# Sparse attention and SwiGLU on one core: batch 2's q and k transposed by PE, later casts and transposes at other places, six output buffers

## The chip, the cores and the metric

The kernel runs on one core of a Trainium2 chip. Five engines work side by side: PE (matmuls, with PEld for its weight loads), DVE (elementwise work), ACT (activations), POOL and SP. In this kernel POOL mostly starts transfers that gather or cast, and SP starts plain transfers and crossbar transposes. Each engine takes its instructions in program order and waits on semaphores for the others. The metric is the device time of one execution in microseconds (us). The kernel before takes 384.35 us, the median of 3 runs (383.87 to 388.22).

## The reference

There are 8 batches of 576 tokens with 8 heads of 64. A token attends to the tokens within 32 places of it; 8 global tokens attend to all and are attended to by all. The result, 4608 tokens of 512 values, goes through a gated feed-forward block.

```
scores = q @ k.T / sqrt(D)                       # per batch and head, 576 x 576
mask   = |i - j| <= 32  or  i is global  or  j is global
attn   = softmax(where(mask, scores, -1e9))
x      = (attn @ v), heads side by side           # 4608 x 512
out    = (silu(x @ w_gate) * (x @ w_val)) @ w_out # 512 -> 1536 -> 512
```

## The kernel before

The feed-forward block is cut into nine **chunks** of 512 tokens. A chunk is 16 **units**: 12 gate units (`gate`, L643: eight matmuls for `pg` and `pv`, then tanh on ACT and two products on DVE that give `h`) and 4 output units (`outp`, L692: twelve matmuls into `po`, a copy by ACT into an `osb` buffer, a transfer by SP to `out`). The units are numbered through from 0; chunk c holds units 16c to 16c + 15.

The attention of a batch is a list of small steps, and these are put into the **gaps** behind the units: `gaps[n]` runs after unit n (L707 to L744). So PE always has feed-forward matmuls between two attention steps. This order, written out by hand, is the order of instructions on every engine. A chunk needs the attention of the tokens that it covers: chunk 3, tokens 1536 to 2047, needs the first 320 tokens of batch 3 (its tiles 0, 1 and 2).

The steps of one batch:

- `step_T` (L330, batches 0 and 1 only): PE transposes k and q of two heads, 24 small transposes. ACT copies the k half into `kT`, DVE the q half into `qT`.
- `step_GT`, `step_S2`, `step_SG`: the global tokens. S2 gives `p2` (global queries), SG gives `pg` (global keys).
- `step_P2T` (L407): `p2` transposed. Batches below XB = 3 do it on PE with an ACT copy; the others by a crossbar transpose started on SP (`p2t`, L410).
- `step_AV2` (L420): the output of the global queries, from `p2t` and `va`.
- `step_S(u)`: banded scores, exp on ACT, band mask on DVE. `step_AV(tp)` and `step_AV8`: the values, then a normalisation on DVE that gives `xa`.
- `step_X(tp)` and `step_X8`: `xa` transposed into `xT`, the feed-forward block's input. Below XB by PE, from XB on by a crossbar transpose on SP (L542, L564).

The inputs of a batch come in three ways. q and k of batches 0 and 1 are loaded and cast by POOL into `k_bf` and `q_bf` (`load_qk_part`, L76; one buffer of each), for `step_T`. q and k of batches 2 to 7 are cast by POOL into a bf16 copy in DRAM with heads side by side (`cast_qk`, L105), and SP transposes the copy into `kT` and `qT` through the crossbar (`transpose_qk`, L113). v goes into `va` by POOL (`load_v`, L96, five blocks; two `va` buffers, so batch b waits for the AV steps of batch b - 2), and SP copies it shifted into `vb` (L123). The rows of the global tokens come by two indirect transfers (`gather`, L221) that POOL then masks (`gather_mask`, L232), waiting for them to land.

For batch b >= 1 the function `later` (L585), at the end of the scores of batch b, starts the transposes of batch b + 2, then gather and mask of batch b + 2 and the cast of batch b + 3; `later_v` does `load_v` of batch b + 2. Batch 2's cast is queued at the very start, behind the weights (L283), its transposes at unit 14, and those of batch 3 at unit 15. Batch 2's steps stand at units 19 to 30, batch 3's from unit 31, batch b's from unit 16(b - 1) - 1.

Work tiles have few buffers: `osb` three (pool `ffnw`, L69), `kT` and `va` two each, `qT` two. PSUM has one double bank for scores (`psc`), one for the rest of attention (`pm`), and four banks for the feed-forward block (`pf`).

Of the kernel before, what the change touches and what calls it, by code (L numbers as in the profile page):

```python
# [9 lines left out]
FP32 = mybir.dt.float32  # L10
# [7 lines left out]
P = 128  # L18
# [8 lines left out]
def kernel(  # L27
# [13 lines left out]
    B, H, S, D = q.shape  # L41
    NG = global_idx.shape[0]
    DM, DF = moe_w_gate.shape
# [7 lines left out]
    LP = 96  # L51
    LJ = S // LP
    KC = S + 2 * WIN
    XB = 3
    STEP = {2: 1.0, 3: 1.08, 4: 1.08, 5: 1.1, 6: 1.1, 7: 1.1}
    W = D + 2

    assert (B, H, S, D, NG, DM, DF) == (8, 8, 576, 64, 8, 512, 1536)
# [78 lines left out]
    loaded = [None] * B  # L137
# [116 lines left out]
    kqms = [None] * B  # L254
# [23 lines left out]
    for i in range(4):  # L278
# [1 line left out]
            out=wo_sb[:, 3 * i : 3 * i + 3, :],  # L280
            in_=moe_w_out[3 * P * i : 3 * P * (i + 1), :].rearrange("(fc p) m -> p fc m", p=P),
        )
    cast_qk(2)  # L283


    mg = const.tile([P, S], BF16)
    mg2 = const.tile([P, KC], BF16)
# [28 lines left out]


    def attention(b):
        ld = loaded[b]
        kT = kT_bufs[b % 2]  # L320
        va = va_bufs[b % 2]
        st = {}
# [7 lines left out]
        def step_T(hp):  # L330
            if hp == 0:
                qTs[b] = bp.tile([P, HP, S], BF16, tag="qT", name="qT")
            if b > 0:
                pool, tag = (pm, "m") if hp == 3 else (psc, "sc")
                pair = pool.tile([P, 2, 1024], BF16, tag=tag, name="ps_t")
            pss = []
            for n, name in enumerate(("k", "q")):
                if b == 0:
                    ps = pf.tile([P, LJ, LP], BF16, tag="f", name="ps_t")
                else:  # L340
                    ps = pair[:, n, 0:S].rearrange("p (j i) -> p j i", j=LJ)
                pss.append(ps)
                src = ld[name]
                for j in range(LJ):
                    for par in range(2):
                        nc.tensor.transpose(  # L346
                            out=ps[64 * par : 64 * par + 64, j, :],
                            in_=src[:, 2 * hp + par, D * j : D * (j + 1)],
                            identity=ident[0:LP, 0:LP],
                        )  # L350
# [4 lines left out]
            nc.vector.tensor_copy(  # L355
                out=qTs[b][:, hp, :].rearrange("p (i j) -> p i j", j=LJ),
                in_=pss[1].rearrange("p j i -> p i j"),
            )
# [46 lines left out]
            nc.vector.tensor_tensor(out=st["p2"], in0=pe, in1=mg2, op=ALU.mult)  # L405

        def step_P2T():  # L407
            if b >= XB:
                st["p2t"] = work.tile([P, 5, P], BF16, tag="p2t", name="p2t")
                nc.sync.dma_start_transpose(out=st["p2t"], in_=st["p2"])  # L410
                return
            ps = mtile([P, 5, P], BF16, "ps_p2t")
            for u in range(5):
                nc.tensor.transpose(
                    out=ps[:, u, :], in_=st["p2"][:, P * u : P * (u + 1)], identity=ident
                )
            st["p2t"] = work.tile([P, 5, P], BF16, tag="p2t", name="p2t")
            nc.scalar.copy(out=st["p2t"], in_=ps)
# [163 lines left out]
        def vb():  # L582
            st["vb"] = load_vb(b)

        def later():  # L585

            if b + 2 < B:
                transpose_qk(b + 2)
                kqms[b + 2] = gather_mask(*gather(b + 2))
            if b + 3 < B:  # L590
                cast_qk(b + 3)

        def later_v():
            if b + 2 < B:
                load_v(b + 2)

        L = lambda f, *a: (lambda: f(*a))
        if b == 0:
            return [
# [5 lines left out]
            ], [L(step_S, 4)], [L(step_AV8), later_v], [L(step_X8)]  # L605
        mid = [
            [L(step_S2), L(step_SG)],
            [L(step_P2T), L(step_S, 0)],
# [6 lines left out]
            [L(step_X, 3), L(step_S, 4), later],  # L615
        ]
        end = [[L(step_AV8), later_v], [L(step_X8)]]
        if b == 1:
            return [
                [L(step_GT)], [], [], [], [L(step_T, 0)], [L(step_T, 1)],  # L620
                [L(step_T, 2), L(step_T, 3), vb],
            ] + mid, end
        if b < XB:
            return [[L(step_GT), vb]] + mid + end
        return [
            [L(step_GT), vb],
            [L(step_S2), L(step_SG)],
# [6 lines left out]
            [L(step_S, 4), L(step_AV, 2), L(step_X, 2), later],  # L634
            [L(step_AV, 3), L(step_AV8), L(step_X, 3), L(step_X8), later_v],
        ]


    def ffn(t0, n):
# [52 lines left out]
        def outp(ts):  # L692
            po = pf.tile([P, DM], FP32, tag="f", name="po")
            for fc in range(NFC):
# [1 line left out]
                    out=po, lhsT=st["h"][:, fc, P * ts : P * (ts + 1)], rhs=wo_sb[:, fc, :],  # L696
                    start=(fc == 0), stop=(fc == NFC - 1),
                )
            osb = ffnw.tile([P, DM], FP32, tag="osb", name="osb")
            nc.scalar.mul(out=osb, in_=po, mul=0.5)  # L700
            r0 = t0 + P * ts
            nc.sync.dma_start(out=out[r0 : r0 + P, :], in_=osb)
# [14 lines left out]
    gaps = dict(enumerate(first))  # L717
    for i, g in enumerate([s4, av8, x8]):
        gaps[1 + i] = g + gaps[1 + i]
    gaps[8].append(lambda: kqms.__setitem__(2, gather_mask(*gather(2))))  # L720
    gaps[10].append(lambda: cast_qk(3))
    gaps[14].append(lambda: transpose_qk(2))
    for i, g in enumerate(last):
        gaps[16 + i] = g
    at = 19.0
    for b in range(2, B):
        steps = attention(b)
        need = (512 - 64 * b + P - 1) // P
# [47 lines left out]
```

## Time and profile before

| | |
|---|---|
| median of 3 runs | 384.35 us |
| the profiled execution, its own time | 384.5 us |
| its span, first to last instruction | 382.8 us |
| mean granted TensorE clock | 0.991 |
| DVE busy | 235.3 us (61%) |
| POOL queue's transfers (q0) | 19.40 MB in 101472 packets |
| SP queue's transfers (q1) | 24.09 MB in 50320 packets |

A row of the timeline gives start, length, engine, line, operation, and the tiles as output<-input; in brackets stands how long the engine had been idle before and what ended the wait. Rows of matmuls can be merged (x4 is four of them), and some matmul records are missing. Matmuls overlap, so the time that a step takes is read from the start of one row to the start of the next. A row of waits gives the engine and line that waited, what ended the wait, the total in us, how many times, and the longest. A row of groups ends in busy time, mean ns of one, and idle time before with what ended it. SPq and POOLq rows are transfers; "to landing" is the time from issue until the data is there.

The first gate of chunk 1 starts at 73.77 us, of chunk 2 at 118.57, of chunk 3 at 163.54, of chunk 4 at 203.40, of chunk 5 at 240.70, of chunk 6 at 279.20 and of chunk 7 at 316.43.

### The profile page before, as it was taken

What the parts mean: (1) busy time and instruction counts of PE and PEld (TensorE: products, weight loads), DVE (VectorE), ACT (ScalarE), POOL (GpSimd) and SP (SyncE); (2) the same over time, 40 slices, a digit from 0 to 9 for tenths busy, and PEclk for the clock granted to TensorE, in tenths of its full rate; (3) what the DMA queues carried; (4) which work ended last, traced back from release to release, by engine and by line L of the source; (5) the groups of instructions that cost most, each with busy time, mean ns of one, the idle gap of its engine ahead of it and who ended that gap; (6) DMA issues with size and microseconds to landing.
All of it is one profiled execution on the core that took longest, in us unless ns stands there. A gap on an engine that the chain in (4) does not pass through costs nothing.

```text
span 382.8 us, 7690 instructions
## 1 busy us (share of the span) xinstructions
PE 346.2 (90%) x3125; PEld 173.5 (45%) x3175; DVE 235.3 (61%) x469; ACT 147.4 (39%) x228; POOL 99.8 (26%) x114
## 2 busy tenths in 40 slices
PE   2678999979899679988999999999999999999995
PEld 2464545434444235433554454345444544444442
DVE  5774885376844639248944993399458926834750
ACT  2633574336334324144414441354154413323321
POOL 8865751609183052450132012000000000000000
PEclk9999999999999969999999999999999999999999
DMA  8999999999989999999299139940350131011002
GB/s 115 115 197 201 185 201 152 145 180 215 170 76 164 228 60 148 138 237 139 28 148 240 29 34 130 212 58 16 99 134 2 29 86 61 0 49 63 0 29 82
DMA packets 151827, 43.98 MB, mean 115 GB/s; under 512 B 138352, under 2 KB 146032, under 8 KB 151792
## 3 DMA queue, kind: packets, MB, share of 16 engines
q0 software_dynamic: 101472, 19.40, 61.8%
q1 hardware_dynamic: 50320, 24.09, 29.6%
q8 instruction: 25, 0.41, 0.5%
q14 instruction: 10, 0.08, 0.1%
HBM read 38.28 MB, written 16.52 MB: 143 GB/s over the span
## 4 chain that ended last, share of the span: by engine, by line
PE 78%; DMA 11%; DVE 5%; issue 3%; ACT 2%; SPq 0%; POOL 0%; DVEq 0%; ACTq 0%; POOLq 0%
PE po L695 24%; PE pg L650 21%; PE pv L650 20%; DMA p2t<-p 5%; PE ps_av L498 3%; DMA qT<-qf 3%; PE ps_s L454 2%; PE ps_av L507 2%; DMA vb<-va 2%; DMA q_bf<-in_q_dram 1%; PE ps_t L346 1%; PE ps_x L552 1%; DVE h L688 1%; DVE gv L684 1%; ACT pe L462 1%
## 5 line engine op out<-in xcount | busy, mean ns | idle before, releaser
L650 PE MATMUL pv<-xT,wv_sb 128*128 128x512 bf16 x420 | 109.2, 381 | 1.9 <-ACT osb L700 1.4
L650 PE MATMUL pg<-xT,wg_sb 128*128 128x512 bf16 x393 | 106.9, 382 | 3.4 <-DVE gv L684 0.8
L684 DVE SCALAR_TENSOR_TENSOR gv<-th,pg 128x512 bf16<-128x512 bf16 x108 | 73.9, 684 | 52.7 <-ACT th L682 52.3
L682 ACT ACTIVATE th<-pg 128x512 bf16<-128x512 f32 x108 | 64.5, 598 | 89.6 <-PE pg L650 78.8
L695 PE MATMUL po<-wo_sb,h 128*128 128x512 bf16 x417 | 94.0, 379 | 2.1 <-issue 1.9
L688 DVE TENSOR_TENSOR h<-gv,pv 128x512 bf16<-128x512 bf16 x108 | 74.3, 688 | 11.7 <-PE ps_av L507 0.5
L650 PEld LDWEIGHTS <-wv_sb 128*128 128x128 bf16 x424 | 41.7, 98 | 52.4 <-issue 3.1
L695 PEld LDWEIGHTS <-h 128*128 128x128 bf16 x432 | 40.8, 98 | 47.0
L700 ACT ACTIVATE osb<-po 128x512 f32<-128x512 f32 x36 | 21.5, 597 | 93.5 <-PE po L695 74.0
L650 PEld LDWEIGHTS <-wg_sb 128*128 128x128 bf16 x424 | 37.6, 98 | 43.8 <-issue 4.8
L101 POOL DMA_DIRECT2D va<-in_v_dram x40 | 37.1, 1195 | 63.8 <-PE ps_av L507 45.1
L462 ACT ACTIVATE pe<-ps_s 128x1024 bf16<-128x1024 f32 (+1 forms) x40 | 37.6, 940 | 19.7 <-PE ps_s L454 19.7
L467 DVE TENSOR_TENSOR pt<-pe,band 128x1024 bf16<-128x1024 bf16 (+1 forms) x40 | 25.4, 635 | 11.0 <-ACT pe L462 10.3
L485 DVE TENSOR_TENSOR xa<-ps_av,den 128x512 bf16<-128x512 f32 (+1 forms) x40 | 25.5, 638 | 1.4
L479 DVE TENSOR_REDUCE den<-ps_av 128x8 f32<-128x16 f32 (+1 forms) x40 | 6.7, 168 | 29.0 <-PE ps_av L507 27.5
L498 PE MATMUL ps_av<-gvt,pg 128*64 128x264 bf16 x128 | 18.8, 303 | 1.0 <-DVE gvt L439 1.0
L507 PE MATMUL ps_av<-vb,pt 128*64 128x66 bf16 x256 | 18.3, 201 | 1.5 <-DMA vb<-va 1.5
L507 PEld LDWEIGHTS <-pt 128*64 128x64 bf16 x512 | 18.4, 117 | 1.9 <-DMA vb<-va 1.7
L454 PEld LDWEIGHTS <-kT 64*128 64x128 bf16 x576 | 11.5, 98 | 16.2 <-issue 15.4
L507 PE MATMUL ps_av<-va,pt 128*64 128x66 bf16 x256 | 18.5, 201 | 0.0
L454 PE MATMUL ps_s<-qT,kT 64*128 64x64 bf16 x576 | 16.4, 197 | 1.8 <-ACT pe L462 1.3
L235 POOL TENSOR_TENSOR kqm<-kg,mka 128x128 bf16<-128x128 f32 x8 | 3.2, 395 | 54.6 <-DMA kg<-in_k_dram,gofs 54.6
(98 smaller groups left out, 210.3 us busy)
## 6 DMA issues: line engine op xcount, KB each, us to landing
out_dram<-osb SPq DMA_DIRECT2D x36, 256.0 KB, 3.3
vb<-va SPq DMA_DIRECT2D x14, 264.0 KB, 4.3
kf<-in_k_dram POOLq DMA_DIRECT2D x6, 576.0 KB, 10.3
qf<-in_q_dram POOLq DMA_DIRECT2D x6, 576.0 KB, 15.2
va<-in_v_dram POOLq DMA_DIRECT2D x24, 128.0 KB, 9.7
va<-in_v_dram POOLq DMA_DIRECT2D x16, 96.0 KB, 8.9
wg_sb<-in_moe_w_gate_dram POOLq DMA_DIRECT2D x3, 512.0 KB, 7.4
wv_sb<-in_moe_w_val_dram POOLq DMA_DIRECT2D x3, 512.0 KB, 9.5
```

The lines of the kernel that those rows point to most:

```text
L101: nc.gpsimd.dma_start(out=va[lo:hi, u, :, 0:D], in_=vs[t0 + lo : t0 + hi])
L454: nc.tensor.matmul(out=ps[:, par, 64 * slot : 64 * slot + 64], lhsT=kT[r : r + 64, hp, 64 * t : 64 * t + P], rhs=qTs[b][r : r + 64, hp, 64 ...
L462: nc.scalar.activation(out=pe, in_=ps[:, :, 0 : 64 * ns].rearrange("p r (s c) -> p r s c", c=64), func=AF.Exp, scale=SCALE,)
L467: nc.vector.tensor_tensor(out=pt.rearrange("p r s c -> p (r s) c"), in0=pe.rearrange("p r s c -> p (r s) c"), in1=bc(band, [[0, 2 * ns], [ ...
L485: nc.vector.tensor_tensor(out=xa.rearrange("p (g h) d -> p g h d", g=g), in0=bc(ps, pst + [[1, D]]), in1=bc(den, [[4, g], [1, 4], [0, D]]) ...
L498: nc.tensor.matmul(out=ps[64 * e : 64 * e + 64, hg], lhsT=st["pg"][:, P * tp + 64 * e : P * tp + 64 * e + 64], rhs=st["gv"].rearrange("p h ...
L507: nc.tensor.matmul(out=ps[64 * e : 64 * e + 64, hg, hl, :], lhsT=pt[:, hl % 2, 4 * (hl // 2) + 2 * (tp % 2) + e, :], rhs=(va if e == 0 els ...
L650: nc.tensor.matmul(out=ps[:, 0:n], lhsT=w[:, cc, P * fc : P * (fc + 1)], rhs=xT[:, cc, t0 : t0 + n], start=(cc == 0), stop=(cc == NCC - 1),)
L682: nc.scalar.activation(out=th[:, 0:n], in_=pg[:, 0:n], func=AF.Tanh, scale=0.5)
L684: nc.vector.scalar_tensor_tensor(out=gv[:, 0:n], in0=th[:, 0:n], scalar=1.0, in1=pg[:, 0:n], op0=ALU.add, op1=ALU.mult,)
L688: nc.vector.tensor_tensor(out=st["h"][:, fc, 0:n], in0=gv[:, 0:n], in1=pv[:, 0:n], op=ALU.mult)
L695: nc.tensor.matmul(out=po, lhsT=st["h"][:, fc, P * ts : P * (ts + 1)], rhs=wo_sb[:, fc, :], start=(fc == 0), stop=(fc == NFC - 1),)
```

## The change

Batch 2 joins batches 0 and 1: its q and k are loaded into `k_bf` and `q_bf` at unit 7 and transposed by PE in four `step_T`, at units 16 to 19. The other steps of batch 2 keep their units (20 to 30). `cast_qk(2)` and `transpose_qk(2)` are gone.

P2T of batch 3 is done by PE too (`XP = 4`); its X steps stay on SP (`XB = 3`).

`later` and `later_v` are gone. Each transfer has a unit of its own, counted from o = 16(b - 1), the first unit of the chunk in which batch b's attention runs: load_v at o - 14, transposes at o - 11, gather at o - 10, cast at o - 24, mask at o - 3 (special places for batches 2 to 4). Gather and mask are no longer called together. The steps of batches 3 to 7 begin at o + 1 in place of o - 1 and end at o + 15 in place of o + 13. `osb` has six buffers.

```diff
+    XQ = 3
     XB = 3
-    STEP = {2: 1.0, 3: 1.08, 4: 1.08, 5: 1.1, 6: 1.1, 7: 1.1}
+    XP = 4
...
-    cast_qk(2)
...
         def step_P2T():
-            if b >= XB:
+            if b >= XP:
...
-        def later():
-
-            if b + 2 < B:
-                transpose_qk(b + 2)
-                kqms[b + 2] = gather_mask(*gather(b + 2))
-            if b + 3 < B:
-                cast_qk(b + 3)
-
-        def later_v():
-            if b + 2 < B:
-                load_v(b + 2)
...
-        if b < XB:
-            return [[L(step_GT), vb]] + mid + end
+        if b < XQ:
+            return [
+                [L(step_T, 0)], [L(step_T, 1)], [L(step_GT), L(step_T, 2)], [L(step_T, 3), vb],
+            ] + mid, end
...
-            osb = ffnw.tile([P, DM], FP32, tag="osb", name="osb")
+            osb = ffnw.tile([P, DM], FP32, tag="osb", name="osb", bufs=6)
...
-    gaps[8].append(lambda: kqms.__setitem__(2, gather_mask(*gather(2))))
-    gaps[10].append(lambda: cast_qk(3))
-    gaps[14].append(lambda: transpose_qk(2))
+    def at(n, f, *a):
+        gaps.setdefault(n, []).append(lambda: f(*a))
+
+    held = {}
+
+    def gather_now(b):
+        held[b] = gather(b)
+
+    def mask_now(b):
+        kqms[b] = gather_mask(*held[b])
+
+    def qk_now(b):
+        loaded[b] = new_qk()
+        load_qk_part(b, loaded[b], 0)
+        load_qk_part(b, loaded[b], 1)
+
+
+    cast_at, tr_at, v_at, g_at, m_at = {3: 12, 4: 25}, {3: 22}, {2: 10}, {2: 8}, {2: 15}
+    at(7, qk_now, 2)
+    two, two_end = attention(2)
     for i, g in enumerate(last):
         gaps[16 + i] = g
-    at = 19.0
-    for b in range(2, B):
+    for i, g in enumerate(two + two_end):
+        gaps[16 + i] = gaps.get(16 + i, []) + g
+    for b in range(XQ, B):
         steps = attention(b)
-        need = (512 - 64 * b + P - 1) // P
-        due = need + 6 if b < XB else need + 5
+        o = 16 * (b - 1)
         for i, g in enumerate(steps):
-            slot = int(at)
+            slot = o + 1 + (16 * i) // len(steps)
             gaps[slot] = gaps.get(slot, []) + g
-            if i == due:
-                assert slot < 16 * b - (b >= XB), (b, slot)
-            at += 1.0 if b < XB else 16.0 / len(steps)
+        if b > XQ:
+            tr_at[b] = o - 16 + 5
+        if b > 4:
+            cast_at[b] = o - 32 + 8
+        v_at[b] = o - 16 + 2
+        g_at[b] = o - 16 + 6
+        m_at[b] = o - 16 + 13
+    for f, w in ((transpose_qk, tr_at), (load_v, v_at), (gather_now, g_at), (mask_now, m_at), (cast_qk, cast_at)):
+        for b, n in w.items():
+            at(n, f, b)
```

More of the change, by code (lines that the diff above doesn't have):

```diff
@@ L318, in attention @@
     def attention(b):
-        ld = loaded[b]
         kT = kT_bufs[b % 2]
@@ L342, in step_T @@
                 pss.append(ps)
-                src = ld[name]
+                src = loaded[b][name]
                 for j in range(LJ):
@@ L604, in attention @@
                 L(step_AV, 3), L(step_X, 2), L(step_X, 3),
-            ], [L(step_S, 4)], [L(step_AV8), later_v], [L(step_X8)]
+            ], [L(step_S, 4)], [L(step_AV8)], [L(step_X8)]
         mid = [
@@ L614, in attention @@
             [L(step_X, 2), L(step_AV, 3)],
-            [L(step_X, 3), L(step_S, 4), later],
+            [L(step_X, 3), L(step_S, 4)],
         ]
-        end = [[L(step_AV8), later_v], [L(step_X8)]]
+        end = [[L(step_AV8)], [L(step_X8)]]
         if b == 1:
@@ L633, in attention @@
             [L(step_AV, 1), L(step_X, 1)],
-            [L(step_S, 4), L(step_AV, 2), L(step_X, 2), later],
-            [L(step_AV, 3), L(step_AV8), L(step_X, 3), L(step_X8), later_v],
+            [L(step_S, 4), L(step_AV, 2), L(step_X, 2)],
+            [L(step_AV, 3), L(step_AV8), L(step_X, 3), L(step_X8)],
         ]
```

## The prediction

> **What bounds the kernel now.** I read the page's busy times and slices first, then the waits of PE, then windows cut at the first gate matmul of each chunk.
>
> ```profile
> PE 346.2 (90%) x3125; PEld 173.5 (45%) x3175; DVE 235.3 (61%) x469; ACT 147.4 (39%) x228; POOL 99.8 (26%) x114
> PE   2678999979899679988999999999999999999995
> ```
>
> PE is busy for 90% of the span; its thin slices are the start, the ninth, and the fourteenth with the fifteenth. So the time is PE's work plus PE's holes, and a change pays where it closes a hole. The holes by cause:
>
> ```profile
> PE ps_av L424 <- DMA p2t<-p: 7.3, 2, 6.0
> PE ps_sg L375 <- DMA qT<-qf: 2.7, 1, 2.7
> PE ps_av L507 <- DMA vb<-va: 1.5, 1, 1.5
> PE pv L650 <- ACT osb L700: 1.4, 2, 0.8
> ```
>
> All four lie in territory that the diff touches. (The next largest, 6.1 us for the first k_bf, is the start, which it leaves alone.) The windows by chunk, first the stretch and its length, then busy times of PE, PEld, DVE, ACT and POOL, the clock, DMA share and GB/s:
>
> ```profile
> 73.77:118.57 44.80, 39.83 (x375) 19.90 (x383) 26.85 (x55) 18.73 (x31) 23.02 (x23) 1.00 1.62 164
> 118.57:163.54 44.97, 38.29 (x339) 18.44 (x344) 25.94 (x50) 15.24 (x23) 11.68 (x12) 0.92 1.46 145
> 163.54:203.40 39.86, 37.17 (x342) 17.97 (x346) 25.27 (x50) 15.05 (x23) 11.60 (x11) 1.00 1.24 141
> 203.40:240.70 37.30, 36.77 (x341) 17.97 (x345) 25.34 (x51) 15.05 (x23) 5.42 (x7) 1.00 0.70 105
> 240.70:279.20 38.50, 37.09 (x339) 17.96 (x344) 24.95 (x50) 15.05 (x23) 0.00 (x0) 1.00 0.47 91
> 279.20:316.43 37.23, 36.70 (x338) 17.91 (x343) 25.29 (x49) 15.32 (x23) 0.00 (x0) 1.00 0.26 64
> ```
>
> These are chunks 1 to 6. Chunks 4 and 6 hold the same work as 2, 3 and 5 (one batch of attention among 16 units) and take 37.3 us. So chunk 2 has 7.7 us to lose, chunk 3 2.6, chunk 5 1.2. Chunk 2's mean clock is 0.92, the others run at 1.00. Chunk 1 has its 4.2 us of qT and vb waits.
>
> **The change, part by part.**
>
> *P2T of batch 3 by PE.* Today batch 3's p2t is a crossbar transpose that PE waits for, and PE is slow after the hole:
>
> ```profile
> 136.44 0.74 PE L424 MATMUL ps_av<-va,p2t 128*32 128x132 bf16 x20 [6.04 <-DMA p2t<-p]
> 137.11 0.61 PE L650 MATMUL pg<-xT,wg_sb 128*128 128x512 bf16 x1
> ...
> 140.35 1.03 PE L650 MATMUL pg<-xT,wg_sb 128*128 128x512 bf16 x4
> ...
> 215.37 0.47 PE L424 MATMUL ps_av<-va,p2t 128*32 128x132 bf16 x20
> 215.78 1.04 PE L650 MATMUL pg<-xT,wg_sb 128*128 128x512 bf16 x4
> 217.51 1.03 PE L650 MATMUL pg<-xT,wg_sb 128*128 128x512 bf16 x3
> ```
>
> Hole 6.04. AV2 then takes 137.11 - 136.44 = 0.67 against 0.41 in batch 5 (215.37 to 215.78), and the gate unit 140.35 - 137.11 = 3.24 against 1.73 (215.78 to 217.51): 1.77 more. Added are five PE transposes and an ACT copy, which batch 1 shows as 0.44 us of PE:
>
> ```profile
> 51.00 0.44 PE L414 MATMUL ps_p2t<-ident,p 128*128 128x128 bf16 x5
> ```
>
> AV2 follows three units later (5.2 us), which covers the copy. Chunk 2: -6.04 - 1.77 + 0.44 = **-7.4 us**.
>
> *Batch 2 by PE.* Gone are its cast from POOL and its two transposes from SP, with the 2.74 us at S2/SG. Its vb, now behind four transposes on SP, is asked for at unit 19, ahead of batch 3's transposes at unit 22: the 1.50 goes. Added are four step_T at units 16 to 19. Batch 1's cost:
>
> ```profile
> 41.36 1.04 PE L650 MATMUL pg<-xT,wg_sb 128*128 128x512 bf16 x3
> ...
> 43.19 0.45 PE L346 MATMUL ps_t<-ident,k_bf 96*64 96x96 bf16 x12
> ...
> 43.83 1.04 PE L650 MATMUL pg<-xT,wg_sb 128*128 128x512 bf16 x4
> ```
>
> Gate plus T is 43.83 - 41.36 = 2.47, less 1.73 for the gate: 0.74 each, a little less where the unit holds attention work anyway; four are 2.8. On PE alone chunk 1 gains 2.74 + 1.50 - 2.8 = 1.4. But each T also gives DVE a copy, and DVE has used these holes to catch up:
>
> ```profile
> L355 DVE COPY qT<-ps_t 128x576 bf16<-128x576 bf16 x8 | 5.9, 753 | 1.9 <-PE ps_t L346 1.8
> ...
> 73.77:106.66 32.89, 28.13 (x301) 14.21 (x306) 24.19 (x47) 15.46 (x24) 11.72 (x13) 1.00 1.76 181
> ...
> 36.90:59.23 22.33, 21.91 (x295) 11.31 (x296) 19.47 (x34) 13.39 (x21) 12.82 (x13) 1.00 1.76 192
> ```
>
> The first window is chunk 1's gate part, the second the like part of chunk 0, where batch 1's T stand and PE has almost no hole at a DVE share of 19.47/22.33 = 87%. Chunk 1 would hold 24.19 + 4 x 0.753 = 27.2 us of DVE; at 87% that is 31.2 us, about the 31.45 that PE's sum gives. The two meet, so some waiting for DVE must come back, most likely where X(0) wants a normalised tile. Between 0 and 1.4 I take **-1.0 us**.
>
> The q/k loads wait on POOL for batch 1's last T (47 us); behind them stand gather, load_v and cast 3, none wanted by PE for 25 us. The loads themselves:
>
> ```profile
> k_bf<-in_k_dram POOLq DMA_DIRECT2D x4, 288.0 KB, 6.5
> q_bf<-in_q_dram POOLq DMA_DIRECT2D x4, 288.0 KB, 7.3
> ```
>
> Issued by 50, they land near 60; T(0) comes at 76. Cost nothing; if that cover went, every us beyond 76 is a us.
>
> *Six osb buffers.* In chunks 3 and 5 ACT's fourth osb waits for an out transfer that stands behind transposes on SP. PE's bare waits are 1.4 us; the windows say more: chunk 5 is 38.50 - 37.23 = 1.3 too long, chunk 3 is 39.86 - 37.30 = 2.56 too long, of which 1.22 is a p2t wait (below). Six buffers cover a chunk's four outputs: **-1.3** in chunk 5, **-1.3** in chunk 3.
>
> *Casts and transposes later.* The slot numbers fix only an order; POOL runs ahead and is held by load_v, whose last blocks wait for AV(3) and AV8 of two batches before. Batch 5's load_v would be held until unit 47 (AV8 of batch 3), then comes the gather, then cast 6:
>
> ```profile
> 158.37 1.64 POOL L101 DMA_DIRECT2D va<-in_v_dram  x2 [4.81 <-PE ps_av L531]
> 160.31 1.04 POOL L225 DMA_INDIRECT kg<-in_k_dram,gofs  x1 [0.30 <-issue]
> 161.66 0.99 POOL L225 DMA_INDIRECT qg<-in_q_dram,gofs  x1 [0.31 <-issue]
> ...
> 167.75 2.28 POOL L108 DMA_DIRECT2D kf<-in_k_dram  x1
> ```
>
> From the first of these to the end of the third is 162.65 - 158.37 = 4.3 us, so cast 6 starts 4.3 us into chunk 3, just where cast 7 stands now (167.75 - 163.54 = 4.2), and cast 7 moves to the same place in chunk 4. Batches 4 and 5 still fetch p2t by DMA, so both now fetch it under a cast. Only batch 4 does today:
>
> ```profile
> 170.16 1.69 SPq L410 DMA_TRANSPOSE p2t<-p  x1
> 208.69 2.25 SPq L410 DMA_TRANSPOSE p2t<-p  x1
> DMA to landing us min/median/max: 10.3/10.3/10.3
> DMA to landing us min/median/max: 7.9/7.9/7.9
> DMA to landing us min/median/max: 4.0/4.0/4.0
> 178.06 0.47 PE L424 MATMUL ps_av<-va,p2t 128*32 128x132 bf16 x20 [1.22 <-DMA p2t<-p]
> ```
>
> The landings are batches 3, 4 and 5, from the tile's windows. PE reached AV2 6.7 us after batch 5's issue (215.37 - 208.69) and would have waited 7.9 - 6.7 = 1.2 under a cast. Against that, the next batch's transposes stand behind p2t on SP (unit 5 after unit 4), and the output transfers are two units further off, so p2t may start sooner. Bounds per batch: 0, and 10.3 - 6.7 = 3.6 if the queue is as full as in batch 3. I take **0.5** for each of batches 4 and 5, near the lower end, since batch 3's 10.3 had two q/k transposes ahead of it on SP. This replaces the 1.22 in chunk 3.
>
> [...]
>
> *Batch 3 to 7 one or two units later.* X(2) of batch 3 goes from unit 43 to 45, and chunk 3's first gate needs it. Between stand two output units:
>
> ```profile
> 152.33 5.13 PE po L695 x23
> L485 DVE TENSOR_TENSOR xa<-ps_av,den 128x512 bf16<-128x512 f32 x32 | 22.1, 691 | 1.1
> xT<-xa SPq DMA_TRANSPOSE x30, 2.6
> ```
>
> 5.1 us of cover, and AV(3) with AV8 besides, against a normalisation of about 1.1 and a transfer of 2.6: nothing, unless it lands over 2 us late. SP's two q/k transposes are off its queue by then (issued at unit 37).
>
> **The sum** against the profiled execution (384.5 us, span 382.8; the median of the runs is 384.35, so it stands for them): -7.4 - 1.0 - 1.3 - 1.3 - 1.22 + 2 x 0.5 = -11.2, so **373.3 us**. Batch 1, the start and chunks 6 to 8 stay.
>
> **Rivals.**
> *p2t under the casts.* Both batches pay 3.6 instead of 0.5: 373.3 + 6.2 = 379.5, within 2% of before. For it: 7.9 and 10.3. Against: both had more ahead of them on SP. At batch 4's price of 1.2 it is 374.7, still my case. Chance 0.13. [...]
> *Chunk 1 becomes DVE's.* No gain from PE transposes, and waits of the size of one normalisation (1.1) at X(0), X(1) and X(2): 373.3 + 1.0 + 3.3 = 377.6. For it: the 87% and 31.2 against 31.45. Against: chunk 0 runs so without holes. Chance 0.08.
> *Slower: batch 2's q and k come late.* Were the four loads served one after another at 10.3 us each, the longest landing quoted above, T(0) would wait from 76 to 50 + 41 = 91: 373.3 + 15 = 388. It decides from a landing at 87 on. For it: DMA share in chunk 1 is over 1.6. Against: landings of 6.5 and 7.3 at the same share, and a cast less in the queue. Chance 0.04.
>
> **How the numbers follow.** About 2% (7.7 us, the line at 376.7) is what a measurement here can tell from no change. My case holds 0.75, all of it below that line. Low end: chunk 1 gains 1.4, p2t costs nothing, 371.9, and a us for AVs that now fall on output units, where DVE idles: 370.9. The high end lies between the DVE rival's 377.6 and the p2t rival's 379.5: 378.0. Faster 0.77 (the forecast and a part of the DVE rival), same 0.18, slower 0.05.
>
> **What would show it.** Right: no PE wait on p2t in chunk 2, clock 1.00 there and 37.6 us for it; chunk 5 at 37.3; no ACT wait on out_dram; chunk 1 near 43.8 with waits on DVE at X(0). Wrong: PE waits on p2t over 2 us in chunks 3 or 4, on k_bf at unit 16, or on xT at the start of chunk 3.

## The result, and the profile after

The changed kernel takes 375.1 us, the median of 4 runs (373.18 to 376.27), beside 386.29 us for the kernel before, the median of 4 runs (383.87 to 388.46). The ratio is 0.9707, with a 95% interval of 0.9617 to 0.9797: faster. The prediction was 373.3 us, with a range of 370.9 to 378.0. Some executions of a kernel fall into a slower state; the ratios here and below leave them out, the medians hold all runs. The profiled execution of the changed kernel takes 376.17 us, its span is 374.5 us.

First the page of the changed kernel: busy times, and the slices of PE and of its granted clock.

```profile
PE 353.1 (94%) x3276; PEld 176.3 (47%) x3276; DVE 241.4 (64%) x473; ACT 150.7 (40%) x233; POOL 98.3 (26%) x116
PE   2688999999999999998999999999999999999996
...
PEclk9999999999999999999999999999999999999999
```

The thin slices in the middle of the span are gone but for one. PE's busy time reads 7 us more than before (353.1 against 346.2), in a span that is 8.3 us shorter. Not all of it is new work: the page has 151 matmuls more (3276 against 3125), of which the change adds 101 (24 in each of the four T of batch 2, five in P2T of batch 3); the other 50 are feed-forward matmuls whose records are missing from the trace of before. The windows by chunk, 1 to 6, have the same columns as those of before:

```profile
76.59:119.64 43.05, 42.39 (x475) 21.96 (x475) 29.57 (x58) 21.06 (x34) 16.00 (x15) 1.00 1.05 117
119.64:157.22 37.58, 37.58 (x351) 18.23 (x349) 24.30 (x45) 16.36 (x25) 6.49 (x7) 1.00 1.17 126
157.22:196.01 38.79, 37.36 (x348) 17.97 (x344) 26.14 (x51) 15.22 (x23) 11.65 (x11) 1.00 1.44 140
196.01:233.87 37.86, 37.38 (x350) 17.98 (x345) 25.95 (x51) 15.22 (x23) 11.68 (x11) 1.00 1.36 143
233.87:271.18 37.31, 37.31 (x350) 17.99 (x345) 25.73 (x51) 15.22 (x23) 4.46 (x6) 1.00 0.55 103
271.18:308.48 37.30, 37.30 (x349) 17.98 (x345) 25.82 (x51) 15.22 (x23) 0.00 (x0) 1.00 0.25 64
```

The holes are read by setting a chunk's length (second column) beside PE's busy time (third): chunks 2, 5 and 6 have none, chunk 3 has 1.43 us, chunk 4 0.48 and chunk 1 0.66. Against before:

| | before | after | difference | predicted |
|---|---|---|---|---|
| up to chunk 1 | 73.77 | 76.59 | +2.82 | 0 |
| chunk 1 | 44.80 | 43.05 | -1.75 | -1.0 |
| chunk 2 | 44.97 | 37.58 | -7.39 | -7.4 |
| chunk 3 | 39.86 | 38.79 | -1.07 | -2.0 |
| chunk 4 | 37.30 | 37.86 | +0.56 | +0.5 |
| chunk 5 | 38.50 | 37.31 | -1.19 | -1.3 |
| chunk 6 | 37.23 | 37.30 | +0.07 | 0 |

Chunks 1 to 6 give 10.8 us, where 11.2 were predicted. Behind them the changed kernel is 0.35 us shorter (382.8 - 316.43 against 374.5 - 308.48). The rest of the difference between the two executions is the start, before anything that the change touches could cost time; it is taken up in the last section.

The three holes that are left have these rows. The first two are PE's waits at AV2 of batches 4 and 5; the next four are POOL's issue of casts 6 and 7 and SP's issue of those two p2t (start, length); the landing is batch 4's, from the tile's window; the last is chunk 1's wait at X(0).

```profile
174.26 0.47 PE L422 MATMUL ps_av<-va,p2t 128*32 128x132 bf16 x20 [1.43 <-DMA p2t<-p]
212.12 0.47 PE L422 MATMUL ps_av<-va,p2t 128*32 128x132 bf16 x20 [0.48 <-DMA p2t<-p]
...
161.64 2.30 POOL L109 DMA_DIRECT2D kf<-in_k_dram  x1
200.42 2.33 POOL L109 DMA_DIRECT2D kf<-in_k_dram  x1
...
164.39 3.08 SPq L408 DMA_TRANSPOSE p2t<-p  x1
203.19 2.06 SPq L408 DMA_TRANSPOSE p2t<-p  x1
...
DMA to landing us min/median/max: 9.8/9.8/9.8
...
101.89 0.40 PE L550 MATMUL ps_x<-ident,xa 128*128 128x128 bf16 x4 [0.66 <-DVE xa L483]
```

Cast 6 starts 4.4 us into chunk 3 and cast 7 4.4 us into chunk 4, where the prediction had put them (4.3), and a p2t is issued 2.8 us behind each. PE reaches AV2 8.4 us after batch 4's issue (174.26 - 1.43 - 164.39), and the landing takes 9.8: 1.4 us of waiting. Batch 5's takes 8.9.

### The profile page after: what moved, and what is told of

Its sections match the earlier page's. It is cut to its first block, busy times and chain, and to the rows that moved or that the text cites. A ratio compares the mean times of both kernels' runs of the same rounds, so it can differ in the third digit from the quotient of the medians.

```text
span 374.5 us, 7948 instructions
## 1 busy us (share of the span) xinstructions
PE 353.1 (94%) x3276; PEld 176.3 (47%) x3276; DVE 241.4 (64%) x473; ACT 150.7 (40%) x233; POOL 98.3 (26%) x116
## 4 chain that ended last, share of the span: by engine, by line
PE 84%; DMA 6%; DVE 5%; ACT 2%; issue 1%; POOL 0%; DVEq 0%; POOLq 0%
PE po L683 25%; PE pg L638 22%; PE pv L638 21%; DMA p2t<-p 5%; PE ps_av L496 3%; PE ps_s L452 2%; PE ps_av L505 2%; PE ps_t L344 2%; DMA q_bf<-in_q_dram 1%; DVE pt L465 1%; PE ps_x L550 1%; DVE h L676 1%; PE pg L657 1%; DVE gv L672 1%; ACT pe L460 1%
## 5 line engine op out<-in xcount | busy, mean ns | idle before, releaser
L638 PE MATMUL pg<-xT,wg_sb 128*128 128x512 bf16 x424 | 109.3, 380 | 1.1 <-ACT xT L556 0.7
L683 PE MATMUL po<-wo_sb,h 128*128 128x512 bf16 x432 | 97.4, 379 | 0.0
L102 POOL DMA_DIRECT2D va<-in_v_dram x40 | 35.2, 912 | 118.4 <-PE ps_av L505 90.8
L109 POOL DMA_DIRECT2D qf<-in_q_dram x5 | 14.1, 2823 | 0.0
```

What stands on the lines that cost most here:

```text
L102: nc.gpsimd.dma_start(out=va[lo:hi, u, :, 0:D], in_=vs[t0 + lo : t0 + hi])
L638: nc.tensor.matmul(out=ps[:, 0:n], lhsT=w[:, cc, P * fc : P * (fc + 1)], rhs=xT[:, cc, t0 : t0 + n], start=(cc == 0), stop=(cc == NCC - 1),)
L683: nc.tensor.matmul(out=po, lhsT=st["h"][:, fc, P * ts : P * (ts + 1)], rhs=wo_sb[:, fc, :], start=(fc == 0), stop=(fc == NFC - 1),)
```

## The experiments

The lengths of chunks 1 to 5 in all profiled executions, each with the start of the first 128x512 gate in chunk 0, from which a late start is seen. "New" kernels are the changed one with an edit, "old" ones the kernel before with an edit.

| kernel | first gate | 1 | 2 | 3 | 4 | 5 |
|---|---|---|---|---|---|---|
| before | 33.93 | 44.80 | 44.97 | 39.86 | 37.30 | 38.50 |
| after | 36.80 | 43.05 | 37.58 | 38.79 | 37.86 | 37.31 |
| u_xp3: new, p2t of batch 3 by crossbar | 37.13 | 43.91 | 37.30 | 38.24 | 38.05 | 37.30 |
| a_xp4: old, P2T of batch 3 by PE | 33.42 | 49.28 | 37.59 | 51.81 | 38.37 | 37.53 |
| u_osb3: new, three osb buffers | 37.53 | 44.11 | 37.58 | 38.87 | 38.12 | 37.30 |
| a_osb6: old, six osb buffers | 33.58 | 46.18 | 45.34 | 41.51 | 37.30 | 37.40 |
| u_b2x: new, batch 2 by crossbar | 37.18 | 41.22 | 37.57 | 37.45 | 37.99 | 37.31 |
| x_nocast: new, no casts 6 and 7 | 33.12 | 43.06 | 37.57 | 37.31 | 37.30 | 37.30 |
| x_castlate: new, casts 6 and 7 later | 33.46 | 43.06 | 37.57 | 37.30 | 37.85 | 37.30 |
| x_qTact: new, batch 2's qT copies on ACT | 34.42 | 43.32 | 37.58 | 38.51 | 37.89 | 37.30 |
| s_only: the new order alone | 33.18 | 48.90 | 37.29 | 37.31 | 38.55 | 37.31 |
| p_only: PE transposes and buffers alone | 34.04 | 44.75 | 37.58 | 38.23 | 37.31 | 37.61 |
| s_best: order, buffers, later casts | 34.10 | 49.34 | 37.30 | 37.30 | 37.30 | 38.91 |
| x_final: new, casts 6 and 7 placed apart | 34.44 | 43.89 | 37.58 | 37.30 | 37.30 | 37.31 |

### What closed chunk 2: P2T on PE, or the order?

In the changed kernel, batch 3's p2t went back to the crossbar:

```diff
-    XP = 4
+    XP = 3
```

> The changed kernel with batch 3's P2T by the crossbar again; all else as changed. Theory A (the 7.4 us of chunk 2 come from taking P2T off the crossbar): PE waits again about 6 us for batch 3's p2t, clock falls, chunk 2 is near 45 us. Theory B (the new order alone, with the q/k transposes behind p2t on SP instead of ahead of it, removes most of the hole, and P2T by PE only the rest): p2t has some 8 us from issue to AV2 and lands in 9 to 10 under cast 5, so PE waits 1 to 2 us, the clock stays at 1.00 and chunk 2 is 38.2 to 39.2 us against 37.58. I expect B.

In the kernel before, only batch 3's P2T went to PE:

```diff
         def step_P2T():
-            if b >= XB:
+            if b >= 4:
```

> The kernel before with batch 3's P2T by PE and nothing else. By the prediction's step chunk 2 falls from 44.97 to 37.6 us, its clock is 1.00, and the other chunks keep their lengths, 44.8, 39.9, 37.3 and 38.5 us (chunk 3 may move by 1 us with the place of its p2t). Rival: the hole moves on, since cast 5 and SP's transposes stay where they are, to the next thing that SP delivers in chunk 2 (vb of batch 3 at AV(0), or X(2) at the start of chunk 3): chunk 2 or 3 longer by 2 us or more than that.

u_xp3 took 377.28 us and a_xp4 393.13 us, one run each, with 383.51 us for the kernel before beside them. u_xp3 has no hole in chunk 2. Its timeline, first the transposes that SP issues there, then AV2; below them SP in the kernel before at the same place:

```profile
128.62 1.25 SPq L408 DMA_TRANSPOSE p2t<-p  x1
129.98 6.17 SPq L116 DMA_TRANSPOSE kT<-kf  x1
...
136.99 0.47 PE L422 MATMUL ps_av<-va,p2t 128*32 128x132 bf16 x20
```

```profile
116.73 6.39 SPq L119 DMA_TRANSPOSE qT<-qf  x1
123.21 1.53 SPq L702 DMA_DIRECT2D out_dram<-osb  x3
...
126.12 1.28 SPq L410 DMA_TRANSPOSE p2t<-p  x1
```

No bracket stands behind the row of AV2: it does not wait. Before, p2t stood on SP behind the q and k transposes of batch 4 and three outputs, and PE arrived 4.28 us after its issue (136.44 - 6.04 - 126.12). In the new order the transposes of batch 4 are queued behind p2t, and PE arrives 8.37 us after the issue; the landing takes 7.9 us, where it took 10.3. So PE comes 4.1 us later after the issue, and the landing is 2.4 us shorter; together they are more than the hole of 6.04. Which part of the new order made the landing shorter was not tried. The order alone covers the transfer, which is more than the expectation gave it, and P2T on PE costs 0.28 us there (37.58 against 37.30).

In the old order, P2T on PE did close chunk 2 (37.59), and chunk 3 became 51.81 us. SP, then PE, of a_xp4 there:

```profile
152.09 6.16 SPq L115 DMA_TRANSPOSE kT<-kf  x1
158.34 7.25 SPq L119 DMA_TRANSPOSE qT<-qf  x1
165.69 1.01 SPq L702 DMA_DIRECT2D out_dram<-osb  x2
...
169.43 1.86 PE L650 MATMUL pv<-xT,wv_sb 128*128 128x512 bf16 x4 [5.82 <-ACT osb L700]
184.13 0.74 PE L424 MATMUL ps_av<-va,p2t 128*32 128x132 bf16 x20 [4.61 <-DMA p2t<-p]
```

SP is held for 13.5 us by two transposes of batch 5. Behind them stand outputs, for whose buffers ACT waits and then PE, and p2t of batch 4. (Chunk 1's 49.28 us is not from this edit, which touches nothing there; it comes from the qT and vb waits of batch 2, 2.94 and 2.85 us.) In this execution the hole of chunk 2 was not removed but paid one chunk later. That is not bound to happen in the old order: p_only, below, has it too and pays nothing of the kind. SP's own rows are not short beside the transfers here: those of the two transposes are 6.16 and 7.25 us long, where the landings take 14.5 and 9.7, and what stands behind them on SP waits that long.

### Six output buffers

```diff
-            osb = ffnw.tile([P, DM], FP32, tag="osb", name="osb", bufs=6)
+            osb = ffnw.tile([P, DM], FP32, tag="osb", name="osb")
```

> The changed kernel with three osb buffers instead of six. Theory A (the buffers removed the waits of ACT's fourth osb): chunks 3 and 5 are about 1.2 us longer again, 40.0 and 38.5 against 38.79 and 37.31. Theory B (the waits went because the q/k transposes no longer stand on SP ahead of the output transfers; the buffers do nothing): chunks 3 and 5 within 0.2 us of the changed kernel's. I expect B in chunk 3 and chunk 5, with up to 0.5 in a chunk where an X transpose holds an output transfer back.

And six buffers alone in the kernel before:

> The kernel before with six osb buffers and nothing else. By the prediction's step chunk 5 falls from 38.5 to 37.3 us. In chunk 3 the wait for osb (about 1.3) goes, but p2t is asked for at the same time and PE comes to it earlier, so part of it returns as a longer p2t wait: chunk 3 between 38.5 and 39.9 us. Rival: no gain, because SP's queue holds the output transfers anyway and the wait moves to the next buffer: chunk 5 stays at 38.5.

u_osb3 took 379.01 us (one run, before 383.51 beside it) and a_osb6 386.35 us (one run, before 393.54 beside it). The windows of chunks 3 and 5, u_osb3's and then a_osb6's:

```profile
159.68:198.55 38.87, 37.37 (x348) 17.98 (x345) 26.16 (x51) 15.23 (x23) 11.68 (x11) 1.00 1.42 140
...
236.67:273.97 37.30, 37.30 (x348) 17.99 (x345) 25.77 (x51) 15.22 (x23) 4.48 (x6) 1.00 0.54 103
```

```profile
164.89:206.40 41.51, 38.92 (x348) 18.47 (x346) 26.09 (x50) 15.33 (x23) 11.62 (x11) 0.96 1.12 135
...
243.70:281.10 37.40, 37.38 (x345) 17.99 (x344) 25.63 (x50) 15.33 (x23) 0.00 (x0) 1.00 0.45 95
```

In the old order the buffers take 1.1 us from chunk 5, near the 1.3 predicted. In chunk 3 they brought nothing in that execution: its p2t wait was 2.59 us in place of 1.22, and the clock 0.96 behind it. In the new order three buffers do as well as six (38.87 against 38.79, 37.30 against 37.31): with the transposes elsewhere on SP, no wait of PE on `osb` is left in these chunks, and the buffers are cover that is not needed.

### The casts over p2t

Casts 6 and 7 were left out; the transposes of batches 6 and 7 read batch 5's copy, so the attention of these two batches is computed with batch 5's q and k.

```diff
-            out=kT[:, :, WIN : WIN + S], in_=flat["k", b].rearrange("s h d -> s (h d)")
+            out=kT[:, :, WIN : WIN + S], in_=flat["k", min(b, 5)].rearrange("s h d -> s (h d)")
...
-        if b > 4:
+        if b == 5:
             cast_at[b] = o - 32 + 8
```

> The changed kernel without the casts of batches 6 and 7; their transposes read batch 5's copy, so the attention of batches 6 and 7 is batch 5's queries and keys. Theory A (p2t of batches 4 and 5 is slow because a cast shares the DMA engines): it lands in 3 to 5 us instead of 9.8 and 8.9, PE's waits of 1.43 and 0.48 us go, chunks 3 and 4 are 37.3 us each against 38.79 and 37.86. Theory B (p2t is slow because of what stands ahead of it on SP's queue, vb and the X transposes): landing stays over 7 us and PE still waits in chunk 3.

And casts 6 and 7 both behind the first block of V's loads:

```diff
-        if b > 4:
+        if b == 5:
             cast_at[b] = o - 32 + 8
-        v_at[b] = o - 16 + 2
+        if b > 5:
+            at(o - 16 + 2, load_v, b, range(0, 1))
+            at(o - 16 + 2, cast_qk, b)
+            at(o - 16 + 2, load_v, b, range(1, 5))
+        else:
+            v_at[b] = o - 16 + 2
```

> The changed kernel with the casts of batches 6 and 7 put between the first and the second block of load_v on POOL, so that they start some 24 us into chunks 3 and 4 instead of 4. If the casts make p2t late and have enough room there: p2t waits of 1.43 and 0.48 us go, chunks 3 and 4 are 37.3 us, the whole 1.9 us shorter. Rival: the cast now meets the X transposes and the output transfers at the end of the chunk, X(1) lands late and the first gate of chunk 4 or 5 waits for xT, which costs 1 us or more and gives the gain back.

x_nocast took 370.52 us and x_castlate 371.31 (one run each, before 393.54 beside them). Without the casts both p2t waits are gone. The tile's line over the transfers of p2t in x_nocast, of which batch 4's is the 4.2, and the windows of chunks 3 and 4:

```profile
DMA to landing us min/median/max: 2.7/2.7/4.2
...
153.54:190.85 37.31, 37.31 (x351) 17.95 (x345) 25.80 (x51) 15.22 (x23) 7.43 (x9) 1.00 0.84 114
190.85:228.15 37.30, 37.30 (x349) 17.95 (x345) 25.85 (x51) 15.22 (x23) 7.13 (x9) 1.00 0.78 113
```

So the casts are what makes p2t late: batch 4's, issued by SP, lands in 9.8 us under cast 6, issued by POOL, and in 4.2 without it. (In the changed kernel p2t of batches 6 and 7, which meets no cast there, lands in 2.7.)

The wait itself has no fixed size. Six profiled executions have the casts at the changed kernel's places (after, u_xp3, u_osb3, u_b2x, x_qTact, s_only). PE waits 1.43, 0.87, 1.50, 0, 1.14 and 0 us in them for batch 4's p2t, and 0.48, 0.67, 0.74, 0.61, 0.52 and 1.18 for batch 5's. In the four with the casts left out or moved (x_nocast, x_castlate, s_best, x_final) it waits for neither.

With the casts later, chunk 3 is whole, but chunk 5's first gate waits for the first tile of x, and this puts the 0.5 us back into chunk 4:

```profile
229.03 1.02 PE L638 MATMUL pg<-xT,wg_sb 128*128 128x512 bf16 x4 [0.48 <-DMA xT<-xa]
```

### X(0) and the copies on DVE

```diff
-            nc.vector.tensor_copy(
+            (nc.scalar.copy if b == 2 else nc.vector.tensor_copy)(
```

> The changed kernel with batch 2's four qT copies on ACT instead of DVE. Theory A (DVE is behind in chunk 1 because of these copies, which is why X(0) waits 0.66 us for xa): the wait falls under 0.2 us and chunk 1 is 42.4 us against 43.05. Theory B (the wait comes from units 22 to 24 themselves, where AV2's and the bands' DVE work falls together): the wait stays, chunk 1 within 0.2 us. ACT gets 2.6 us more; if ACT becomes late, T(1) or S2 waits for it.

x_qTact took 373.8 us (one run, before 393.54 beside it). Taking four copies of 0.75 us from DVE left the wait at X(0) as it was:

```profile
99.52 0.40 PE L550 MATMUL ps_x<-ident,xa 128*128 128x128 bf16 x4 [0.66 <-DVE xa L483]
```

The reason that the prediction gave for this wait, DVE's added copies, falls. The same wait stands in kernels where PE transposes nothing of batch 2, here a_osb6 and s_only:

```profile
101.42 0.40 PE L552 MATMUL ps_x<-ident,xa 128*128 128x128 bf16 x4 [0.63 <-DVE xa L485]
```

```profile
103.89 0.40 PE L551 MATMUL ps_x<-ident,xa 128*128 128x128 bf16 x4 [0.66 <-DVE xa L484]
```

Of the 14 profiled executions only before and a_xp4 do not have it, and there PE has waited for vb (1.50 and 2.85 us) shortly ahead of X(0). So the prediction was right that DVE catches up in such a hole, and the 0.66 us are the price of closing it. What DVE does meanwhile is the work of these units themselves: in x_qTact the timeline marks no idle stretch on it from 90.85 us until this normalisation ends at 99.46.

### Batch 2 by PE

In the changed kernel, batch 2 went back to the cast and the crossbar, at the old places:

```diff
+    cast_qk(2)
...
-                [L(step_T, 0)], [L(step_T, 1)], [L(step_GT), L(step_T, 2)], [L(step_T, 3), vb],
+                [], [], [], [L(step_GT), vb],
...
-    cast_at, tr_at, v_at, g_at, m_at = {3: 12, 4: 25}, {3: 22}, {2: 10}, {2: 8}, {2: 15}
-    at(7, qk_now, 2)
+    cast_at, tr_at, v_at, g_at, m_at = {3: 12, 4: 25}, {2: 14, 3: 22}, {2: 10}, {2: 8}, {2: 15}
```

> The changed kernel with batch 2's q and k cast by POOL behind the weights and transposed by SP at unit 14, as before; no step_T for batch 2; all else as changed. Theory A (the sum: PE transposes cost 2.6 to 2.8 us, the qT wait was 2.7 and the vb wait 1.5): the qT wait comes back with 2 to 3 us, the vb wait does not (vb now stands behind two transposes, not four), the DVE wait of X(0) goes; chunk 1 is 43 to 44 us against 43.05, so batch 2 by PE is worth between 0 and 1 us. Theory B (the whole 1.75 us of chunk 1 is due to batch 2 by PE): chunk 1 near 44.8.

It took 375.65 us (one run, before 383.51 beside it), and chunk 1 was shorter than in the changed kernel and than either theory gave, 41.22 us. That looks as if PE's transposes were a loss of 1.8 us. But two later runs with the same edit among others, s_only and s_best (below), had a chunk 1 of 48.9 and 49.3 us. The wait for qT, of u_b2x and then of s_only:

```profile
88.49 0.43 PE L374 MATMUL ps_sg<-qT,gT 128*32 128x288 bf16 x8 [0.36 <-DMA qT<-qf]
```

```profile
88.81 0.67 PE L374 MATMUL ps_sg<-qT,gT 128*32 128x288 bf16 x8 [5.69 <-DMA qT<-qf]
89.41 1.89 PE L639 MATMUL pg<-xT,wg_sb 128*128 128x512 bf16 x4
```

In both, the matmuls start between 88.4 and 88.9 us. The landing of qT does not follow PE: issued at 81.31 us in u_b2x it took 7.1 us, issued at 76.51 in s_only it took 12.3. u_b2x's PE started late (first gate 37.18) and met it almost by chance, s_only's started early (33.18) and waited 5.69 us, after which the gate's four matmuls took 1.89 us in place of 1.04, at a granted clock of 0.50 in that stretch. At an early start the changed order of chunk 1 ends at 115.97 (x_nocast, which up to there is the changed kernel), s_only's at 121.91; at a late start the changed kernel's ends at 119.64 and u_b2x's at 119.41. So in these executions batch 2 by PE was worth 5.9 us at an early start, and at a late one nothing by these ends and a loss of 1.8 by the chunk's length. It takes the landing of qT out of chunk 1. The kernel before has this dependence too: chunk 1 took 44.80, 49.28 and 46.18 us in it and in its two edits a_xp4 and a_osb6, of which a_xp4 changes nothing in that chunk. In the old order with batch 2 on PE (p_only, below) it took 44.75: the qT and vb waits are gone there too, but PE waits 1.52 us at GT for DVE's copy of qT.

### The two halves, each alone

s_only is the changed order with none of the other parts (batch 2 and p2t of batch 3 by crossbar, three osb buffers). p_only is the kernel before, with its order, and batch 2 and P2T of batch 3 by PE and six osb buffers; with batch 2 on PE, its cast and its two transposes leave POOL and SP:

```diff
-    cast_qk(2)
...
-            if b >= XB:
+            if b >= 4:
...
-            return [[L(step_GT), vb]] + mid + end
+            return [[L(step_T, 0)], [L(step_T, 1)], [L(step_T, 2)], [L(step_T, 3), L(step_GT), vb]] + mid + end
...
-    gaps[14].append(lambda: transpose_qk(2))
+    gaps[7].append(lambda: qk_now(2))
```

s_best is s_only with six buffers and later casts, cast 6 behind the first block of V's loads and cast 7 behind the third.

> Only the order is changed: the changed kernel with batch 2 by cast and crossbar, batch 3's P2T by the crossbar and three osb buffers, as before; casts, transposes, load_v, gather and mask at their new units. Theory A (the order is the whole gain, PE's parts cost 1.8 us in chunk 1 and 0.3 in chunk 2): chunks 1 to 5 are 41.2, 37.3, 37.5 to 38.8, 38.0 and 37.3 us; the time is 1 to 2 us below the changed kernel, 372 to 375, ratio to before at most 0.97. Theory B (the prediction's: P2T by PE is worth 7.4 us of chunk 2, the buffers 2.6): chunk 2 near 45, chunks 3 and 5 1.2 us longer, about 383.

> Only the parts other than the order are changed: the kernel before with batch 2 transposed by PE (loads at unit 7, T at units 16 to 19), batch 3's P2T by PE and six osb buffers; casts, transposes, load_v, gather and mask where they were. Theory A (order): the hole of chunk 2 moves on; chunk 2 is 37.6, but chunk 3 waits over 3 us for p2t of batch 4 behind the transposes of batch 5, and chunk 1 or 3 is longer than in the changed kernel by that; the time is 377 to 386. Theory B (the prediction's steps): every named hole but p2t of batch 4 goes, chunks 1 to 5 are 43.8, 37.6, 38.5, 37.3, 37.3, the time 373 to 375, as with the whole change.

> The order alone with six osb buffers, and cast 6 put behind the first block of load_v, cast 7 behind its third. If p2t's waits in chunks 3 and 4 come from the casts, and a cast behind AV(2) no longer meets X(1): chunks 1 to 5 are 41.2, 37.3, 37.3, 37.3 and 37.3 us, 2 to 4 us below the changed kernel's sum, the time 369 to 373, ratio to before about 0.96. Rival: cast 7 lands too late for the transposes at unit 85 or meets p2t of batch 6, and chunk 5 gets 1 us or more.

Beside the kernel before (385.79 us, the median of 7 runs) s_only took 378.66 us, ratio 0.9733 (0.9623 to 0.9843), p_only 377.66 us, ratio 0.9778 (0.9713 to 0.9843), and s_best 380.34 us, ratio 0.9811 (0.9728 to 0.9893). Each of the three intervals reaches above 0.98, so these times alone do not put any of them a clear 2% below before. Chunk 2's windows, of s_only and then of p_only:

```profile
121.91:159.20 37.29, 37.29 (x345) 17.96 (x344) 24.22 (x45) 15.82 (x24) 6.51 (x7) 1.00 1.19 131
```

```profile
118.57:156.15 37.58, 37.58 (x352) 18.25 (x350) 25.65 (x50) 15.87 (x24) 11.55 (x11) 1.00 1.32 155
```

Each half alone closes chunk 2's hole: it is 7.68 us shorter with the order, 7.39 with the PE half, and 7.39 with both. They cure the same wait, so their gains don't add; by the times they gain 2.7% and 2.2% alone and 2.9% together, with intervals that overlap. What the order alone leaves is chunk 1's qT wait (48.90 us), which the PE half takes away; with it s_only missed the 372 to 375 us that its expectation gave.

The hole that was expected to move on to chunk 3 in p_only did not: PE waits 0.85 us for p2t there, where a_xp4 waits 5.82 for an osb buffer and 4.61 for p2t. The order on SP is the same there, but POOL starts cast 5 at another time. That cast, then SP's transposes of its copy, in p_only:

```profile
124.45 2.28 POOL L108 DMA_DIRECT2D kf<-in_k_dram  x1
...
148.11 2.16 SPq L115 DMA_TRANSPOSE kT<-kf  x1
150.36 3.09 SPq L119 DMA_TRANSPOSE qT<-qf  x1
```

In a_xp4 POOL has waited 18.26 us for the gathered rows of batch 4, and the cast starts at 142.06, 10 us ahead of the transposes in place of 24:

```profile
142.06 2.27 POOL L108 DMA_DIRECT2D kf<-in_k_dram  x1
```

SP is held for 5.3 us in p_only and for 13.5 in a_xp4. That the distance to the cast is the reason fits these rows, but was not tried by itself; p_only also has six osb buffers, and batch 2's cast and crossbar transposes are gone.

s_best missed its 369 to 373 us, by a qT wait of 6.00 us in chunk 1 and because its casts went one step too far: cast 7 then stands over p2t of batch 6, which PE waits 1.53 us for, and chunk 5 is 38.91 us.

### The casts placed apart

The last run took what the others had shown: the changed kernel, with cast 6 behind the first and cast 7 behind the second block of V's loads.

```diff
-        if b > 4:
+        if b == 5:
             cast_at[b] = o - 32 + 8
-        v_at[b] = o - 16 + 2
+        if b > 5:
+            m = 1 if b == 6 else 2
+            at(o - 16 + 2, load_v, b, range(0, m))
+            at(o - 16 + 2, cast_qk, b)
+            at(o - 16 + 2, load_v, b, range(m, 5))
+        else:
+            v_at[b] = o - 16 + 2
```

> The changed kernel with cast 6 issued behind the first block of V's loads of its batch and cast 7 behind the second, about one block and two blocks later on POOL than in the changed kernel. Theory (the casts of batches 6 and 7 run over the transposes of the probabilities of batches 4 and 5 and make them late by 1.4 and 0.5 us): those two waits go; chunk 3 falls from 38.8 to about 37.3 us, chunk 4 from 37.9 to about 37.3, chunk 5 stays at 37.3; the sum of chunks 1 to 5 falls by about 2 us, the time to 371 to 374.5 us, a ratio to the kernel before of about 0.963. Rival: a later cast collides with the next thing on its way, either the transpose of batch 6's probabilities (chunk 5 longer by about 1.6 us, as in the order-alone run with later casts) or the first transposes of x of the next batch (chunk 4 still 37.9, as when both casts are one block later); then only chunk 3's 1.5 us are gained or less, and the time isn't told apart from the changed kernel's.

It took 373.19 us, the median of 6 runs (371.88 to 376.58), beside 389.32 us for the kernel before, the median of 11 runs; the ratio is 0.9627 (0.9572 to 0.9683). Its windows of chunks 3 and 4:

```profile
156.29:193.59 37.30, 37.30 (x349) 17.97 (x345) 25.80 (x51) 15.21 (x23) 11.74 (x11) 1.00 1.12 124
193.59:230.89 37.30, 37.30 (x348) 17.99 (x345) 25.81 (x51) 15.21 (x23) 11.57 (x11) 1.00 1.14 135
```

Chunks 2 to 5 have no hole left; they sum to 149.49 us against the changed kernel's 151.54. POOL issues cast 6 at 180.13 us and cast 7 at 222.53, behind AV2 of their chunks (171.8 and 209.1). The gain of 2.05 us is read in the chunks; the two ratios overlap, so the times alone don't tell this kernel from the changed one. Chunk 1 was 43.89 us, not 43.06 as expected: T waits 0.77 us there for DVE's copy of qT. The same wait stands in u_xp3 and u_osb3 (0.78 and 0.98) and not in the other new kernels. In all three DVE's copy itself has waited for ACT's copy of kT (1.27, 1.27 and 1.48 us); what holds ACT there is open.

## Why the prediction was right, and where it was not

**The sum** held: 10.8 us in chunks 1 to 6 where 11.2 were forecast. The median, 375.1, lies 1.8 us above the forecast. The profiled execution's surplus over it, 376.17 - 373.3 = 2.9 us, is as large as its late start, 2.87 us at the first gate; the 0.4 that the chunks fell short and the 0.35 gained behind them cancel. The sum held better than its terms: chunk 1 brought 0.75 more than was forecast, chunk 3 0.95 less.

**Chunk 2, -7.39 for -7.4.** The size was right: the hole and the slow matmuls behind it went, five PE transposes came. The step that failed is the cause. "P2T of batch 3 by PE" was costed alone, against the order of before, while the change reorders the same queue. u_xp3 and s_only show that the order closes the hole without it, so in the changed kernel P2T on PE is worth nothing and costs 0.28 us. p_only shows that P2T on PE closes it without the order; in a_xp4 it did so only for the waits to come back in chunk 3. The prediction saw that in before two q and k transposes stood ahead of p2t on SP, and used it only for the landings of batches 4 and 5.

**Chunk 1, -1.75 for -1.0.** The waits of 2.74 and 1.50 us went, 0.66 came back at X(0), as foreseen in place though not in cause (x_qTact, a_osb6). The rows of S2 and of the first gate behind AV(0), before and then after, tell the terms apart:

```profile
83.25 0.46 PE L393 MATMUL ps_s<-kT,gT 128*32 128x320 bf16 x8
98.50 1.04 PE L650 MATMUL pg<-xT,wg_sb 128*128 128x512 bf16 x4
```

```profile
88.73 0.46 PE L391 MATMUL ps_s<-kT,gT 128*32 128x320 bf16 x8
99.33 1.04 PE L638 MATMUL pg<-xT,wg_sb 128*128 128x512 bf16 x4
```

From the chunk's start to S2 it is 9.48 us before and 12.14 after: the four T cost 2.66, where 2.8 was taken. From S2 to that gate it is 15.25 and 10.60: closing the two waits brought 4.65, where their own 4.24 were taken. From there to the end the changed kernel needs 0.24 more, where 0.4 was left for DVE; the X(0) wait is in it, and the other way GT of batch 3, about 0.3 us, which now stands in chunk 2. So no term was far off, and all three erred to the same side. What the step missed is that the qT wait of before has no fixed size (2.74 us in before, 2.94 in a_xp4, 3.5 in a_osb6); the gain is larger where a run of before waits longer.

**Six buffers, -1.3 in chunks 3 and 5.** The reading of before was right (a_osb6: 1.1 us in chunk 5), the credit was not: in the new order u_osb3 has the same gain with three. Chunk 3's share of 1.3 was not lost, the order brought it.

**p2t of batches 4 and 5, 0.5 us each.** The mechanism was right and the place too; batch 4's term was mis-sized, 1.43 us where 0.5 was taken, batch 5's 0.48. Some luck is in both, as the six executions above show (0 to 1.50 and 0.48 to 1.18). This is nearly all of what chunk 3 lacks (0.93 of 0.95). The landing under the cast was 9.8 us, near the 10.3 that the prediction set aside as due to SP's queue; in x_nocast, with the same order on SP and no cast, it is 4.2, so the cast makes most of it. What kept the price down is the slack: 8.4 us, not 6.7.

**At nothing:** the q and k loads of batch 2 came in time and X(2) of batch 3 two units later cost nothing, as said; no wait on `k_bf` or `xT` stands at those places. The sign that ACT would no longer wait on `out_dram` was not quite met: one wait of 2.0 us is left, in the last chunk at 365.7 us, where PE does not wait for it.

**The rivals.** p2t at 3.6 us each did not come, and chunk 1 did not become DVE's: one wait of 0.66 us stands there, not three of 1.1. Batch 2's loads were not late.

## What to carry to other kernels

When a change moves work off a queue and reorders the same queue, cost each part against the new order as well as the old: two parts that cure one wait don't add (7.68 and 7.39 us of chunk 2 alone, 7.39 together), and one of them alone may only move the wait to the next stage, as it did in one of two kernels here. A wait whose end is set by other transfers had no fixed size here (0 to 1.50 us for batch 4's p2t, with the casts at the same places); a single profile of either kernel says little about it. A transfer that is to be moved is placed by what else is short of slack along its way, here p2t on one side (a wait of 1.43 us) and the first tile of x on the other (0.48).

## What was not expected of the hardware

The start has two lengths. In the first gates of chunk 0 (the 384-wide ones, 16 matmuls) the kernel before and the changed kernel differ, in windows of just these matmuls, first before's and then after's:

```profile
28.48:31.08 2.60, 2.60 (x17) 1.56 (x17) 0.11 (x1) 0.00 (x0) 2.44 (x4) 1.00 1.24 188
```

```profile
29.06:33.95 4.89, 4.89 (x16) 2.33 (x16) 0.00 (x0) 0.00 (x0) 3.44 (x5) 1.00 1.27 192
```

The same work takes 2.60 or 4.89 us, a factor of 1.88, while the column of the granted clock says 1.00 in both. Of the 14 profiled executions four have the long start (after, u_xp3, u_osb3, u_b2x; first gate at 36.8 to 37.5 us) and ten do not (33.1 to 34.4), four of these with the changed kernel's own chunk 0 (x_nocast, x_castlate, x_qTact, x_final); so the change does not force it. Whether it makes it more frequent cannot be told: none of the four executions in the old order has it. What decides between the two lengths, no row here shows. That the spread of the changed kernel's runs (373.2 and 374.0, and two of 376.2 and 376.3) has this cause is likely by its size; shown it is only for the one that was profiled.
